# Operand loads of attention backward: larger pieces, requested by SP instead of GpSimd

## The chip, the cores and the metric

The program runs on one core of a Trainium2 chip. The metric is the device time of one execution in microseconds (us), lower is better. TensorE is called PE, VectorE DVE, ScalarE ACT, GpSimd POOL and SyncE SP, as in the profile. PE, DVE, ACT and POOL compute; SP here only requests DMA transfers.

## The reference

The kernel computes the output and nine gradients of a transformer block with adaptive layer norm (2048 tokens, width 512, 32 heads of 16, feed-forward width 1792), bfloat16 in and out. The part that matters here is the backward pass of the attention:

```
scores = einsum('bhqd,bhkd->bhqk', q, k) * scale
p = softmax(scores, axis=-1)
o = einsum('bhqk,bhkd->bhqd', p, v)
_out, _vjp = jax.vjp(_f, A_x, A_wqkv, A_wo, B_w1, B_b1, B_w2, B_b2, c, w_mod)
_grads = _vjp(grad_out)
```

For each head the backward pass forms P again from Q and K, dP from dO and V, then dS = P * dP (the row sums of dP are folded into two extra columns of dO and V), and from these dV = P^T dO, dK = dS^T Q and dQ = dS K.

## The kernel before

The program has a forward part with the feed-forward block and its backward mixed in (to about 1165 us in the profile), the attention backward `attn_bwd` (about 1165 to 2390 us, lines 1431 to 1655), and a last part for the projection gradients (`phase6`). The change lies in `attn_bwd`.

**Loops.** The 32 heads are 8 quads `g` of four heads. A quad is worked off as two pairs of heads, `jp` = 0 and 1, so there are 16 pairs. In a pair, `c` runs over four chunks of 512 keys and `ib` over 16 blocks of 128 queries, in groups of `G` = 4 blocks (`ib0`): 16 groups in a pair, 256 in all. For each block and each of the two heads `a`, PE computes the scores `st` (line 1608), ACT takes their exponential into `pu` (1611), PE computes `dp` (1522) one block late, and DVE multiplies the two into `ds` (1526). In some groups one of the eight products of a group goes over ACT to POOL instead (1540, 1541).

**The transposes.** dQ needs `ds` transposed. When a group of four blocks has its `ds`, SP requests one crossbar transfer for it (`dma_start_transpose`, line 1549, in `dS`): a [128 x 4096] bfloat16 tile, 1 MB, from SBUF to SBUF into one of five buffers `dsT` (one of them is a part of the tile `keep`). In every fourth group PE turns 4 of the 32 blocks itself (1565), and 28 are left to the transfer. PE reads two groups of transposed `ds` together, in `dq` (line 1484, accumulator `accq`): `dq` items wait in the list `pendq` until more than eight are there, so the two groups k and k+1 are read from the start of group k+4 on, two items after every even block. PE's instructions are in an order written by hand and are run in that order, and so are those of SP and POOL.

**The loads.** The operands of the next pair or quad are read from DRAM while the current pair is worked on. `load_group(g)` (1391) gives the pieces for a quad: `QT` and `dOT` (features on the partitions, 32 partitions for a head, of which 16 or 18 hold data), and `K`, `Q`, `dO` (tokens on the partitions). `pair_pieces(g, jp)` (1423) gives the four pieces for a pair, of K and V, which go into the tile `kvm` (`masked`). `load_wmt` and `wq_pieces` give pieces of weights for the last part. In the last pair 16 pieces of `xhat1` are loaded. Half of a quad's pieces belong to each of its two pairs.

The list `pieces` of a pair is spread evenly over its 16 groups. This is the place, lines 1594 to 1597:

```
while pieces and ((total - len(pieces)) * SC * ST <= m * G * total or m == SC * ST // G - 1):
    if last:
        nc.gpsimd.tensor_copy(tick[:], last[7][0:1, 0, 0, 0:1])
    nc.gpsimd.dma_start(*pieces.pop(0))
```

`m` is the group's number in the pair, and `last` the block before. The copy to `tick` reads one element of the `ds` of the group before, so that POOL does not run ahead with the loads. The first loads of all, for the first pair, are requested by SP at line 933, ahead of `attn_bwd`.

Of the kernel before, what the change touches and what calls it, by code (L numbers as in the profile page):

```python
# [19 lines left out]
P = 128  # L20
DH = 16
# [4 lines left out]
def chunks(total, size):  # L26
    out = []
    s = 0
    while s < total:
        w = min(size, total - s)  # L30
        out.append((s, w))
        s += w
    return out
# [72 lines left out]
class K:  # L106
# [1284 lines left out]
    def load_group(self, g):  # L1391

        S, ST, qp = self.S, self.ST, self.qp
        tm = {"K": self.ktm_d, "Q": self.qtm_d, "dO": self.dOp_d}
        fm = {"QT": (self.QTq_d, DH), "dOT": (self.dOTq_d, DH + 2)}
        width = {n: S if n in fm else ST * P if n == "K" else ST * 4 * DH for n in (*fm, *tm)}
        if g < 2:
            T, o = {}, 0
            for n, e in width.items():
                if g:  # L1400
                    T[n] = qp.tile([P, e], BF16, name=f"{n}g")[:]
                elif n == "K":
                    T[n] = self.keep[:, :e]
                else:
                    T[n] = self.q0[:, o:o + e]
                    o += e
            self.Tq[g] = T
        T, pieces = self.Tq[g % 2], []
        for n, (src, rows) in fm.items():
            if g < 2:  # L1410
                pieces += [(T[n][:, s0:s0 + sw], src[g, :, s0:s0 + sw]) for (s0, sw) in chunks(S, 1024)]
            else:
                pieces += [(T[n][r:r + rows, :], src[g, r:r + rows, :]) for r in range(0, P, 32)]
        for n, src in tm.items():
            pieces += [(T[n][:, a:a + 256], src[g, :, a:a + 256]) for a in range(0, width[n], 256)]
        return {n: t if n in fm else t.rearrange("p (st w) -> p st w", st=ST) for n, t in T.items()}, pieces

    def wq_pieces(self, t):
# [3 lines left out]

    def pair_pieces(self, g, jp):
        pieces = []
        for n, src, sh, rows in (("KT", self.KTq_d, 0, DH), ("VT", self.VTq_d, 2, DH + 2)):
            for j in (2 * jp, 2 * jp + 1):
                r = 32 * ((j + sh) % 4)
                pieces.append((self.masked[n][j % 2][r:r + rows, :], src[g, r:r + rows, :]))
        return pieces

    def attn_bwd(self):
# [7 lines left out]
        tc, nc = self.tc, self.nc  # L1439
# [24 lines left out]
        def turn(g, jp, kvT, s0):  # L1464

            if kvT is None:
                return turn_q(g, jp)
            h0 = 4 * g + 2 * jp
            n = ST // 2
            tp = stp.tile([P, n, P], BF16, name="st")  # L1470
            for st in range(n):
                nc.tensor.transpose(tp[:, st, :], kvT[:, (s0 + st) * P:(s0 + st + 1) * P], self.ident[:])
            v = tp[:].rearrange("p s (t a e) -> p t s a e", t=2, a=2)
            for t, dst in enumerate((self.dk_t, self.dv_t)):
                d = dst[:, s0:s0 + n, h0 * DH:(h0 + 2) * DH].rearrange("p s (a d) -> p s a d", a=2)
                nc.scalar.copy(d, v[:, t, :, :, 0:DH])
# [40 lines left out]
        def dP(u, a):  # L1517

            (T, g, jp, c, ib, kvT, pu, dsg, i, grp) = u
            rd = slice(64 - 64 * jp, 128 - 64 * jp)  # L1520
            dp = dpp.tile([P, 512], F32, name="dp")
            nc.tensor.matmul(dp[:], lhsT=T["dOT"][rd, ib * P:(ib + 1) * P],  # L1522
                             rhs=masked["VT"][a][rd, 512 * c:512 * (c + 1)], start=True, stop=True)
            if a == 1 and i == 1 and off(c, ib):
                return dp
            nc.vector.tensor_tensor(dsg[:, i, a], dp[:], pu[:, a, :], ALU.mult)  # L1526

        def odd(c, ib):
            return (c * SC + ib // G) % 2 == 1

        def no_turn(c, ib):
            return ib // G > 0
# [4 lines left out]
        def dP_pool(u, dp):  # L1537
            (T, g, jp, c, ib, kvT, pu, dsg, i, grp) = u
            f = (self.junk6, self.csq)[(c * SC + ib // G) % 2]
            nc.scalar.copy(f[:], dp[:])  # L1540
            nc.gpsimd.tensor_tensor(dsg[:, i, 1], f[:], pu[:, 1, :], ALU.mult)  # L1541
# [23 lines left out]
                nc.tensor.transpose(tp[:, b, :], dsg[:, 0, 0, b * P:(b + 1) * P], self.ident[:])  # L1565
            nc.scalar.copy(dsT[:, 0:4 * P], tp[:].rearrange("p b k -> p (b k)"))

        tick = self.tick
        wmt = self.load_wmt()
        T = self.T0  # L1570
        last = None
        for g in range(NQ):
            for jp in range(2):
                if jp == 0:
                    if g + 1 < NQ:
                        Tn, later = self.load_group(g + 1)
                    else:
                        Tn, later = None, self.wq_pieces(1) + wmt[2 * g + 1:]
                    cut = len(later) // 2 if Tn else len(later)
                    pieces = self.pair_pieces(g, 1) + wmt[2 * g:2 * g + 1] + later[:cut]  # L1580
                    later = wmt[2 * g + 1:2 * g + 2] + later[cut:]
                elif g + 1 < NQ:
                    pieces = self.pair_pieces(g + 1, 0) + later
                else:
                    pieces = [(self.xhat1_6[:, st, :], self.xhat1_d.rearrange("(st p) d -> p st d", p=P)[:, st, :])
                              for st in range(ST)]
                kvT = kvp.tile([P, S], BF16, name="kvT")
                end = (g, jp) == (NQ - 1, 1)
                total = len(pieces)
                for c in range(SC):  # L1590
                    c0 = 512 * c
                    for ib0 in range(0, ST, G):
                        m = c * (ST // G) + ib0 // G
                        while pieces and ((total - len(pieces)) * SC * ST <= m * G * total or m == SC * ST // G - 1):
                            if last:
                                nc.gpsimd.tensor_copy(tick[:], last[7][0:1, 0, 0, 0:1])
                            nc.gpsimd.dma_start(*pieces.pop(0))
                        dsg, grp = self.dsp.tile([P, G, 2, 512], BF16, name="ds"), []
                        for i in range(G):
                            ib = ib0 + i  # L1600
                            q = slice(ib * P, (ib + 1) * P)
                            if turnq and i == 3 and m >= (7 if turnq[0][2] is None else 2):
                                turn(*turnq.pop(0))
                            pu = self.pup.tile([P, 2, 512], BF16, name="pu")
                            for a in range(2):
                                stt = stp.tile([P, 512], F32, name="st")
                                rs = slice(64 * jp, 64 * jp + 64)
                                nc.tensor.matmul(stt[:], lhsT=T["QT"][rs, q], rhs=masked["KT"][a][rs, c0:c0 + 512],  # L1608
                                                 start=True, stop=True)
                                held = dP(last, a) if last else None  # L1610
                                nc.scalar.activation(pu[:, a, :], stt[:], ACT.Exp, scale=self.scale)  # L1611
                                if held is not None:
                                    dP_pool(last, held)
                                if a == 0 and i % 2 == 1 and odd(c, ib) and len(pend) >= 4:
                                    kv_two(1)
                            if last:
                                dS(last)
                            last = (T, g, jp, c, ib, kvT, pu, dsg, i, grp)
                            if i % 2 == 1 and len(pend) >= 4:
                                kv_two(1 if odd(c, ib) else 2)  # L1620
                            elif i % 2 == 0 and len(pendq) > 2 * G:
                                for _ in range(4 if end else 2):
                                    dq(pendq.pop(0))
                            if i == 2:
                                turn_ds(dsg, grp, no_turn(c, ib), end and m > 2)
            T = Tn
# [339 lines left out]
```

## Time and profile before

| | |
|---|---|
| time, median of 3 runs | 2515.87 us (2509.63 to 2516.81) |
| span of the profiled execution | 2498.5 us |
| median less span | 17.4 us |
| attention backward in the profile | about 1165 to 2390 us |
| busy share of the whole span | PE 96%, ACT 91%, DVE 68%, POOL 30% |
| crossbar transfers of `ds` (line 1549) | 256 |
| loads at line 1597, copies to `tick` at line 1596 | 260 and 259 |

The span runs from the first to the last instruction of one profiled execution; the time of a run also holds what lies around it, here 17.4 us against the median. In the rows below, `PE accq L1484 <- DMA dsT<-ds` means that the instruction on PE that writes `accq` at line 1484 waited for the DMA that writes `dsT` from `ds`. SPq and POOLq are the queues of requests on SP and POOL. The row of a DMA request on SP lasts as long as SP is held by it; the transfer lands later, and "DMA to landing" counts from the request's start. q1 is the hardware queue that SP uses, q0 the software queue of POOL.

### The profile page before, as it was taken

The numbers are of one execution on the slowest core, as the hardware profiler recorded it, in microseconds if no ns is written. First come the engines' busy times: TensorE is split into PE (matmuls) and PEld (weight loads), VectorE is DVE, ScalarE is ACT, GpSimd is POOL, SyncE is SP. The second block draws the span as 40 slices with busy tenths as digits, with TensorE's granted clock in tenths as the row PEclk, the third lists the DMA queues.
The fourth block names the chain that finished last, engine by engine and source line by source line (L and its number), as shares of the span: only waits on it lengthen the run. The fifth ranks groups of instructions, "written<-read, shape, count | busy, mean of one in ns | idle before, by whom it ended". The sixth has DMA issues, their size and how long they took to land.

```text
span 2498.5 us, 67897 instructions
## 1 busy us (share of the span) xinstructions
PE 2410.2 (96%) x26211; PEld 1061.6 (42%) x26439; DVE 1695.0 (68%) x3487; ACT 2283.1 (91%) x3757; POOL 753.5 (30%) x1337
## 2 busy tenths in 40 slices
PE   8999999999999999999999999999999999999998
PEld 4555555555555555583233332333333333333343
DVE  6222322422332343576999999999999999999957
ACT  7999999999999997534999999999999999999945
POOL 2344531220131022245222323322333222322223
PEclk9999999999999999999999999999999999999999
DMA  4589661541243045499999999999999999999997
GB/s 166 135 179 208 169 125 47 132 100 40 92 114 98 23 123 147 110 199 216 232 235 233 232 227 231 237 234 231 230 235 239 234 230 236 234 233 236 238 217 192
DMA packets 1293547, 454.13 MB, mean 182 GB/s; under 512 B 1236948, under 2 KB 1261398, under 8 KB 1293222
## 3 DMA queue, kind: packets, MB, share of 16 engines
q1 hardware_dynamic: 1252422, 344.68, 71.8%
q0 software_dynamic: 38720, 104.04, 13.9%
q8 instruction: 207, 3.39, 0.6%
q10 hardware_dynamic: 2080, 1.05, 0.2%
q14 instruction: 118, 0.97, 0.1%
HBM read 75.83 MB, written 64.49 MB: 56 GB/s over the span
## 4 chain that ended last, share of the span: by engine, by line
PE 49%; ACT 35%; DMA 7%; issue 5%; DVE 3%; POOL 1%; SPq 1%; ACTq 0%; DVEq 0%; POOLq 0%
ACT pu L391 26%; PE st L1608 17%; PE acckv L1459 8%; ACT pu L1611 6%; DMA dsT<-ds 5%; PE accq L1484 5%; PE st L388 4%; PE dp L1522 2%; PE accbank L322 2%; PE dps L1050 2%; PE dp L1659 1%; PE st L1754 1%; ACT csq L1540 1%; PE pps L1237 1%; DVE ds L1526 1%
## 5 line engine op out<-in xcount | busy, mean ns | idle before, releaser
L1526 DVE TENSOR_TENSOR ds<-dp,pu 128x512 bf16<-128x512 f32 x1888 | 1166.0, 682 | 34.6 <-PE dp L1522 19.1
L1611 ACT ACTIVATE pu<-st 128x512 bf16<-128x512 f32 x2048 | 1073.8, 666 | 34.7 <-PE st L1608 21.3
L391 ACT ACTIVATE pu<-st 128x1024 bf16<-128x1024 f32 x992 | 912.1, 1077 | 4.2 <-PE st L388 3.7
L388 PE MATMUL st<-QTm,KTq 128*128 128x512 bf16 x1859 | 560.9, 377 | 27.1 <-ACT pu L391 6.1
L322 PEld LDWEIGHTS <-pu 128*128 128x128 bf16 x8192 | 346.7, 96 | 236.1 <-issue 3.0
L1522 PE MATMUL dp<-kvm,q 64*128 64x512 bf16 x1024 | 365.0, 384 | 2.0 <-DVE ds L1526 0.7
L322 PE MATMUL accbank<-Vaug,pu 128*128 128x17 bf16 x8192 | 357.4, 171 | 8.3 <-ACT Vaug L522 1.1
L1522 PE MATMUL dp<-kvm,dOTg 64*128 64x512 bf16 x1024 | 363.6, 383 | 0.3
L1608 PE MATMUL st<-kvm,q 64*128 64x512 bf16 x1024 | 349.4, 382 | 5.4 <-ACT pu L1611 0.2
L1608 PE MATMUL st<-kvm,QTg 64*128 64x512 bf16 x1024 | 348.1, 381 | 6.5
L1541 POOL TENSOR_TENSOR ds<-csq,pu 128x512 bf16<-128x512 f32 x128 | 147.2, 1150 | 627.0 <-ACT csq L1540 553.6
L388 PEld LDWEIGHTS <-KTq 128*128 128x128 bf16 x1984 | 188.4, 96 | 176.9 <-issue 124.8
L1459 PE MATMUL acckv<-ds,Qg 128*16 128x512 bf16 x1024 | 176.2, 382 | 0.3
L1459 PE MATMUL acckv<-pu,q 128*16 128x512 bf16 x1024 | 176.3, 383 | 0.0
L1459 PE MATMUL acckv<-ds,q 128*16 128x512 bf16 x1024 | 176.2, 383 | 0.0
L1459 PE MATMUL acckv<-pu,dOg 128*16 128x512 bf16 x1024 | 176.0, 382 | 0.0
L302 POOL DMA_DIRECT2D QTm<-QTq_d x124 | 63.1, 511 | 341.5 <-PE st L388 320.0
L1608 PEld LDWEIGHTS <-q 64*128 64x128 bf16 x1024 | 67.0, 94 | 163.5 <-issue 150.6
L1608 PEld LDWEIGHTS <-QTg 64*128 64x128 bf16 x1024 | 67.1, 94 | 160.6 <-issue 145.7
L329 DVE RECIPROCAL rl<-accbank 128x4 f32<-128x4 f32 x128 | 22.9, 179 | 158.3 <-PE accbank L322 158.2
L1522 PEld LDWEIGHTS <-q 64*128 64x128 bf16 x1024 | 88.8, 93 | 52.9 <-issue 43.3
L1522 PEld LDWEIGHTS <-dOTg 64*128 64x128 bf16 x1024 | 88.2, 93 | 52.9 <-issue 43.8
(390 smaller groups left out, 3055.1 us busy)
## 6 DMA issues: line engine op xcount, KB each, us to landing
KTq<-KTq_d POOLq DMA_DIRECT2D x24, 512.0 KB, 3.9
duT_d<-auT POOLq DMA_DIRECT2D x3, 1792.0 KB, 7.9
aT_d<-rT POOLq DMA_DIRECT2D x3, 1792.0 KB, 11.5
KTq_d<-KTq SPq DMA_DIRECT2D x32, 128.0 KB, 2.1
QTq_d<-ev_fm SPq DMA_DIRECT2D x32, 128.0 KB, 4.3
ktm_d<-ev_tm POOLq DMA_DIRECT2D x32, 128.0 KB, 2.5
VTq_d<-vT POOLq DMA_DIRECT2D x4, 1024.0 KB, 6.3
dx<-dx_d SPq DMA_DIRECT2D x16, 256.0 KB, 4.6
```

The source lines that it names most:

```text
L302: nc.gpsimd.dma_start(QTm[j][32 * j:32 * j + 32, :], self.QTq_d[g, 32 * j:32 * j + 32, 512 * qc:512 * (qc + 1)])
L322: nc.tensor.matmul(acc[:, a, sub, :], lhsT=pu[:, a, sub * P:(sub + 1) * P], rhs=Vaug[:, kb, h, :], start=(kb == 0 and a == 0 and sub == 0) ...
L388: nc.tensor.matmul(stt[:, a, :], lhsT=KT[:, kb * P:(kb + 1) * P], rhs=QTm[2 * jp + a][:], start=True, stop=True)
L391: nc.scalar.activation(pu[:], stt[:], ACT.Exp, scale=self.scale)
L1050: nc.tensor.matmul(pt[:], lhsT=a[st], rhs=g_tm[:, st, :], start=(st == 0), stop=(st == ST - 1))
L1459: nc.tensor.matmul(acckv[r:r + DH, :], lhsT=T[n][:, ib, col:col + DH], rhs=src[:, a, :], start=(ib == 0), stop=(ib == ST - 1))
L1484: nc.tensor.matmul(accq[r:r + 32, o:o + 256], lhsT=T["K"][:, 4 * c + sub, col:col + 32], rhs=v[:, r // 32 % 2 * 2:r // 32 % 2 * 2 + 2, 4 * ...
L1522: nc.tensor.matmul(dp[:], lhsT=T["dOT"][rd, ib * P:(ib + 1) * P], rhs=masked["VT"][a][rd, 512 * c:512 * (c + 1)], start=True, stop=True)
L1526: nc.vector.tensor_tensor(dsg[:, i, a], dp[:], pu[:, a, :], ALU.mult)
L1541: nc.gpsimd.tensor_tensor(dsg[:, i, 1], f[:], pu[:, 1, :], ALU.mult)
L1608: nc.tensor.matmul(stt[:], lhsT=T["QT"][rs, q], rhs=masked["KT"][a][rs, c0:c0 + 512], start=True, stop=True)
L1611: nc.scalar.activation(pu[:, a, :], stt[:], ACT.Exp, scale=self.scale)
```

## The change

The loads of lines 1594 to 1597 are requested by SP, so they stand in the same queue as the crossbar transfers. The copy to `tick` is gone: the place in SP's order now holds a load back. The pieces are larger: `K`, `Q` and `dO` in 1024 columns instead of 256 (for quads 1 to 7), `QT` and `dOT` (quads 2 to 7) in two pieces instead of four. Since such a piece now spans two heads, it also reads the unused partitions between them: 48 rows for `QT` instead of two times 16, 64 for `dOT` instead of two times 18. The V pieces have 32 rows instead of 18. There are 152 loads instead of 260.

```
-        fm = {"QT": (self.QTq_d, DH), "dOT": (self.dOTq_d, DH + 2)}
+        fm = {"QT": (self.QTq_d, 32 + DH), "dOT": (self.dOTq_d, 64)}
...
-                pieces += [(T[n][r:r + rows, :], src[g, r:r + rows, :]) for r in range(0, P, 32)]
+                pieces += [(T[n][r:r + rows, :], src[g, r:r + rows, :]) for r in range(0, P, 64)]
         for n, src in tm.items():
-            pieces += [(T[n][:, a:a + 256], src[g, :, a:a + 256]) for a in range(0, width[n], 256)]
+            pieces += [(T[n][:, a:a + w], src[g, :, a:a + w]) for a, w in chunks(width[n], 1024 if g else 256)]
...
-        for n, src, sh, rows in (("KT", self.KTq_d, 0, DH), ("VT", self.VTq_d, 2, DH + 2)):
+        for n, src, sh, rows in (("KT", self.KTq_d, 0, DH), ("VT", self.VTq_d, 2, 32)):
...
-        tick = self.tick
...
-                            if last:
-                                nc.gpsimd.tensor_copy(tick[:], last[7][0:1, 0, 0, 0:1])
-                            nc.gpsimd.dma_start(*pieces.pop(0))
+                            nc.sync.dma_start(*pieces.pop(0))
```

The order of PE, ACT and DVE is the same in both kernels. SP's and POOL's change. These are SP's requests at the start of pair (g, jp) = (3, 0) before, only crossbar transfers into the buffers `dsT` and `keep`:

```order
L1549 DMA_TRANSPOSE keep<-ds 128x32x128
L1549 DMA_TRANSPOSE dsT_19897<-ds 128x32x128
L1549 DMA_TRANSPOSE dsT_19898<-ds 128x28x128
L1549 DMA_TRANSPOSE dsT_19899<-ds 128x32x128
L1549 DMA_TRANSPOSE dsT_19900<-ds 128x32x128
L1549 DMA_TRANSPOSE keep<-ds 128x32x128
L1549 DMA_TRANSPOSE dsT_19897<-ds 128x28x128
```

And SP at the same place now (line 1597 of before is 1594 here); `kvm` takes the K and V pieces of the next pair:

```order
L1549 DMA_TRANSPOSE keep<-ds 128x32x128
L1594 DMA kvm<-KTq_d 16x2048
L1549 DMA_TRANSPOSE dsT_19897<-ds 128x32x128
L1549 DMA_TRANSPOSE dsT_19898<-ds 128x28x128
L1594 DMA kvm<-KTq_d 16x2048
L1549 DMA_TRANSPOSE dsT_19899<-ds 128x32x128
L1549 DMA_TRANSPOSE dsT_19900<-ds 128x32x128
L1594 DMA kvm<-VTq_d 32x2048
L1549 DMA_TRANSPOSE keep<-ds 128x32x128
L1549 DMA_TRANSPOSE dsT_19897<-ds 128x28x128
```

A load now stands ahead of about every second crossbar transfer, right behind the one before. On POOL, at the same place before, pairs of a copy and a load stood between the products of line 1541 (`csq` holds what ACT copied there):

```order
L1541 TENSOR_TENSOR ds<-csq,pu 128x512
L1596 COPY tick<-ds 1x1
L1597 DMA kvm<-KTq_d 16x2048
L1596 COPY tick<-ds 1x1
L1597 DMA kvm<-KTq_d 16x2048
L1541 TENSOR_TENSOR ds<-csq,pu 128x512
L1596 COPY tick<-ds 1x1
L1597 DMA kvm<-VTq_d 18x2048
```

Now POOL has the products alone in the attention backward:

```order
L1541 TENSOR_TENSOR ds<-junk_19880,pu 128x512
L1541 TENSOR_TENSOR ds<-csq,pu 128x512 x6
L1541 TENSOR_TENSOR ds<-junk_19880,pu 128x512
L1541 TENSOR_TENSOR ds<-csq,pu 128x512 x2
L1541 TENSOR_TENSOR ds<-junk_19880,pu 128x512
```

All copies and loads have left POOL's order there, and the order of its products is kept.

## The prediction

> **What bounds the kernel now.** I read the busy times by stretch first. The columns are the stretch, its length, PE's busy time with its instructions, the granted clock, the DMA share and GB/s.
>
> ```profile
> 1165.00:1250.00 85.00, 79.52 (x766) 0.98 1.05 212
> 1250.00:1400.00 150.00, 148.45 (x1618) 1.00 1.21 234
> 1400.00:1550.00 150.00, 146.52 (x1580) 1.00 1.21 229
> 1550.00:1700.00 150.00, 148.09 (x1608) 1.00 1.23 236
> 1700.00:1850.00 150.00, 148.22 (x1608) 1.00 1.21 232
> 1850.00:2000.00 150.00, 147.75 (x1604) 1.00 1.22 236
> 2000.00:2150.00 150.00, 148.63 (x1610) 1.00 1.20 233
> 2150.00:2300.00 150.00, 148.37 (x1618) 1.00 1.21 232
> 2300.00:2385.00 85.00, 82.18 (x889) 1.00 1.20 239
> sum 1220.00, PE 1197.72; mean PE 133.08
> ```
>
> PE is busy in 1197.7 of 1220.0 us. The change moves no instruction of PE, ACT or DVE, so it can take away at most the 22.3 us in which PE stands still, 0.9% of the time. The DMA engines are never quiet either. Next, the waits of PE in this stretch (total, times, longest), and what the crossbar requests look like on SP:
>
> ```profile
> PE accq L1484 <- DMA dsT<-ds: 7.4, 12, 2.9
> PE dp L1522 <- DVE ds L1526: 0.7, 3, 0.3
> ```
>
> ```profile
> L1549 SPq DMA_TRANSPOSE dsT<-ds x208: 3490/4262/6457, 1173.4 to 2377.8; - x104
> L1549 SPq DMA_TRANSPOSE keep<-ds x48: 3550/4204/5392, 1192.2 to 2300.7; - x48
> DMA to landing us min/median/max: 5.1/7.2/9.0
> ```
>
> Of PE's idle time only 7.4 us are put down to a DMA: PE wants a transposed tile that has not landed, twelve times. The 256 requests start (2377.8 - 1173.4) / 255 = 4.72 us apart, and a median one holds SP for 4.26 us of that. So SP and the transfers behind it run nearly as full as PE.
>
> The longest wait shows what happens. These are single requests on SP, one from each of four short windows, then PE at 1217, the chain of waits there, and POOL's loads just before:
>
> ```profile
> 1173.45 3.53 SPq L1549 DMA_TRANSPOSE dsT<-ds  x1
> ...
> 1187.45 4.03 SPq L1549 DMA_TRANSPOSE dsT<-ds  x1
> ...
> 1206.13 5.37 SPq L1549 DMA_TRANSPOSE dsT<-ds  x1
> ...
> 1211.60 6.46 SPq L1549 DMA_TRANSPOSE dsT<-ds  x1
> ```
>
> ```profile
> 1217.22 0.40 PE L1484 MATMUL accq<-dsT,keep 128*32 128x256 bf16 x6 [2.90 <-DMA dsT<-ds]
> ```
>
> ```profile
> 1206.13 11.04 DMA dsT<-ds
> ```
>
> ```profile
> 1195.98 0.59 POOL L1597 DMA_DIRECT2D QTg<-QTq_d  x1
> ...
> 1197.78 0.54 POOL L1597 DMA_DIRECT2D QTg<-QTq_d  x1 [0.26 <-issue]
> ...
> 1204.86 0.58 POOL L1597 DMA_DIRECT2D dOTg<-dOTq_d  x1
> ...
> 1207.00 0.54 POOL L1597 DMA_DIRECT2D dOTg<-dOTq_d  x1 [0.26 <-issue]
> ```
>
> Undisturbed, 32 blocks (1 MB) hold SP 4.03 us and 28 blocks 3.53. While POOL's loads of 256 KB run (128 x 1024 bfloat16), the same request takes 5.37 and then 6.46 us. The tile requested at 1206.13 came after 11.04 us, and PE had waited 2.90 of them, so it was due 11.04 - 2.90 = 8.1 us after its request. The median landing is 7.2 us. **The spare time is thus about 0.9 us**, and whatever delays one transfer by more makes PE wait.
>
> **The change part by part.** *POOL.* 259 copies and 260 requests go away. PE gains nothing from that, since POOL's products wait for ACT, not for POOL:
>
> ```profile
> POOL ds L1541 <- ACT csq L1540: 553.6, 115, 8.1
> ...
> POOL kvm L1597 <- PE dp L1522: 8.5, 25, 0.6
> ```
>
> ```profile
> L1596 POOL COPY tick<-ds 1x1 bf16<-1x1 bf16 x259 | 45.7, 177 | 106.6 <-DVE ds L1526 106.6
> ```
>
> The copies are 45.7 us of work on an engine that is 30% busy. Value 0.
>
> *Bytes.* A normal first pair of a quad now has nine loads: two K pieces of 64 KB (16 rows of 4 KB), two V pieces of 128, 96 of weights, two of QT of 192, two of dOT of 256: 1376 KB. Over all 152 loads the shapes add up to 23424 KB, against 19632 KB in 260 before, 19% more. At the crossbar's own 4.03 us per 1024 KB, 1376 KB is 5.4 us of transfer in a pair.
>
> *SP.* What a plain load costs on SP shows at line 933, where SP itself loads the first pair (min/median/max in ns):
>
> ```profile
> L933 SPq DMA_DIRECT2D kvm<-KTq_d x2: 354/378/402, 1140.1 to 1140.5; - x2
> L933 SPq DMA_DIRECT2D kvm<-VTq_d x2: 368/399/430, 1140.9 to 1142.9; - x2
> L933 SPq DMA_DIRECT2D q<-QTq_d x2: 357/510/664, 1143.4 to 1151.6; - x2
> L933 SPq DMA_DIRECT2D q<-dOTq_d x2: 443/606/769, 1152.3 to 1155.0; - x2
> ```
>
> Nine loads: 2 x 0.38 + 2 x 0.40 + 0.4 + 2 x 0.51 + 2 x 0.61 = 4.2 us of SP. A pair lasts 16 x 4.72 = 75.5 us, and its 16 transfers undisturbed hold SP for 12 x 4.03 + 4 x 3.53 = 62.5. The loads add between 4.2 us (the requests alone) and 4.2 + 5.4 = 9.6 us (if the transfer time is paid on SP as well): 66.7 to 72.1 us. Before, the contention with POOL's loads was already in SP's rows: 16 x 4.26 = 68.2. So SP does not run full on the average, at either end. I take 62.5 + 5.4 + 1 = 69, about as before, since a request is made while the queue still has work.
>
> The Trainium skill, Perfetto Trace Analysis, section "DMA Instruction — HWDGE (DVE, Sync)", says that such a row runs until the descriptors are made and that the data movement is not in it; by that alone a load would cost SP its own row and the pair would need the 66.7. The rows above differ: the same request took 4.03 us and 6.46 us, so here a full queue is in the row.
>
> *One load ahead of one transfer.* SP has 4.72 - 4.03 = 0.69 us free in a group. A 256 KB load costs between 0.51 us (the lower of its two median rows) and 0.61 + 1.0 = 1.6 us; I take 1.0, its transfer time. The transfer behind it is then 0.3 us late, less than the 0.9 us to spare, and nine loads in 16 groups leave a free group behind most of them, in which 0.69 us are won back. Queued behind the load are all later transfers, and PE waits for those. The four loads that caused the 2.90 us wait now stand at groups 9, 11, 13 and 15 and not four in eleven us.
>
> *Waits on SP.* A load of K waits for the last scores of the pair before, which PE runs before SP comes to that request; POOL's requests waited there for at most 0.6 us. 0, at most 2 x 0.6 in a pair, which the free time takes up.
>
> *Sum.* Of the 7.4 us the 2.9 go, and of the other 4.5 (eleven waits of 0.4 us) I let about half go: -5 us. Span 2498.5 - 5 = 2493.5; with the 17.4 us around it 2511 us against 2515.87, or -0.2%. That is below 0.3%, about what a measurement of this kernel can tell from no change.
>
> **The rivals.** *The queue does not catch up (slower).* If a large load costs more than the 2 x 0.69 = 1.38 us that SP wins back until the next, the lag grows over the second half of each pair. For it speak the rows of the last part, where SP has loads of 256 KB between smaller transposes:
>
> ```profile
> 2394.08 1.36 SPq L1737 DMA_TRANSPOSE dqT<-dv_t  x1
> ...
> 2437.72 1.03 SPq L1741 DMA_DIRECT2D dx<-dx_d  x2
> 2438.84 1.24 SPq L1737 DMA_TRANSPOSE dqT<-dk_t  x1
> 2440.13 4.08 SPq L1737 DMA_TRANSPOSE dqT<-dv_t  x1
> ```
>
> Two loads take 1.03 us, and the second transpose behind them 4.08 instead of 1.36: (1.03 + 2.72) / 2 = 1.9 us for one. Four such loads leave 4 x 0.5 = 2 us at the pair's end, 1.1 beyond the spare time, in 14 pairs 16 us; the last pair has a load of 128 KB in each group, at half of 1.9 less 0.69 = 0.26 us each 4 us more: 2536. Against it: POOL's loads run in that stretch too, and may be what the 4.08 us shows.
>
> *Nothing changes (2516).* The same 16 DMA engines move the same bytes and a fifth more, and PE's late tiles stay late for the transfer time, not for the requester. The Trainium skill, DMA: Bandwidth & Descriptors, section "Issuing engines are not separate DMA queues", says just this: requests from any engine interleave on the same engines, and only time on the requester is saved. By that rule the time stays. The trace agrees so far that loads from POOL slow SP's transfers.
>
> *All of it goes (faster).* If the transfers pace the loop in ways that no wait shows, PE's idle time from 1250 to 2300 us, 1050 - 1036.0 = 14 us, goes with the 2.9: 2516 - 17 = 2499. For it: SP is held 4.26 of 4.72 us, and the profile puts waits of SP down to the copy that goes:
>
> ```profile
> SPq L1549 <- DVE ds L1526: 440.0, 182, 5.8
> SPq L1549 <- POOL tick L1596: 313.9, 149, 5.3
> ```
>
> ```profile
> 1195.87 0.18 POOL L1596 COPY tick<-ds 1x1 bf16<-1x1 bf16 x1
> ```
>
> ```profile
> 1196.63 4.56 SPq L1549 DMA_TRANSPOSE dsT<-ds  x1
> ```
>
> Against it: here the copy ended at 1196.05, 0.58 us before the request that is said to have waited for it, so DVE's last product released it; and only 7.4 us of PE's waits name a DMA.
>
> **How the numbers follow.** Forecast (2508 to 2514): 0.49, of which 0.10 beyond -0.3%. Nothing: 0.15. All of it: 0.18. Slower: 0.18. Faster by over 0.3% is then 0.18 + 0.10 = 0.28, within 0.3% is 0.39 + 0.15 = 0.54, slower 0.18. The likeliest time is 2511; the range reaches half into the faster rival and half into the slower one, 2503 to 2528.
>
> **What would show it.** Right: the waits of PE for `dsT` fall from 7.4 to about 3 us and the 2.9 us wait near the start is gone; the undisturbed 4.03 us becomes the usual row at line 1549; a load's row on SP is 0.4 to 1.0 us; the requests at line 1549 come 4.70 us apart. Wrong: rows of line 1549 behind a load of 6 us and more, waits for `dsT` that gather at the ends of the pairs (the slower rival), or waits that stay at 7 us (nothing).

## The result and the profile after

The changed kernel takes 2535.64 us (median of 4 runs, 2532.37 to 2540.76), the kernel before beside it 2512.75 us (4 runs, 2509.32 to 2516.81): a ratio of 1.0101 with a 95% interval of 1.0077 to 1.0125. It is slower by 23 us. The prediction, 2511 us in a range up to 2528, was wrong.

The profiled execution after has a span of 2530.6 us at a time of 2532.37 us. In each of its four runs the time is only 1.8 us above the span. The 17.4 us that the prediction took as lying around the span of before were thus mostly another thing: its profiled execution was faster than the median of the runs. The spans of the two pages differ by 32.1 us, the medians by 22.9, and some 9 us of what the two traces show is this difference between executions.

**The crossbar transfers.** Line 1549 after (min/median/max in ns, first and last start):

```profile
L1549 SPq DMA_TRANSPOSE dsT<-ds x208: 3515/4238/8600, 1171.2 to 2409.0; - x104
L1549 SPq DMA_TRANSPOSE keep<-ds x48: 3509/4172/5563, 1190.0 to 2329.7; - x48
...
DMA to landing us min/median/max: 5.2/6.5/9.8
```

They start (2409.0 - 1171.2) / 255 = 4.85 us apart instead of 4.72 before. These 0.13 x 255 = 33 us are the whole difference of the spans, so all of it is in the attention backward. The rows on SP did not become shorter (median 4.24 us for 4.26). From request to landing, however, a transfer is now faster, 6.5 us for 7.2. What is late is the request. This is SP over 38 us (start, duration, request; x2 are two in a row):

```profile
1437.38 4.27 SPq L1549 DMA_TRANSPOSE dsT<-ds  x1
1441.70 0.57 SPq L1594 DMA_DIRECT2D keep<-ktm_d  x1
1442.37 8.19 SPq L1549 DMA_TRANSPOSE dsT<-ds  x2
1450.60 0.57 SPq L1594 DMA_DIRECT2D keep<-ktm_d  x1
1451.28 5.68 SPq L1549 DMA_TRANSPOSE dsT<-ds  x1
1457.06 4.20 SPq L1549 DMA_TRANSPOSE keep<-ds  x1
1461.32 0.57 SPq L1594 DMA_DIRECT2D q<-qtm_d  x1
1461.98 8.54 SPq L1549 DMA_TRANSPOSE dsT<-ds  x2
1470.58 0.58 SPq L1594 DMA_DIRECT2D q<-dOp_d  x1
1471.27 4.43 SPq L1549 DMA_TRANSPOSE dsT<-ds  x1
```

Each row begins within 0.12 us of the end of the one before: SP has no free time here. Over the whole stretch, 231 of 255 transfers start within 0.25 us of the end of the request ahead of them; before it was 124. A load adds its row of 0.57 us and a second gap of about 0.1 us:

```profile
L1594 SPq DMA_DIRECT2D kvm<-KTq_d x30: 502/528/577, 1162.9 to 2262.2; - x30
...
L1594 SPq DMA_DIRECT2D q<-dOTq_d x6: 582/590/601, 1382.9 to 2016.8; - x6
```

A piece of 16 KT rows (64 KB) and one of 64 dOT rows (256 KB) hold SP almost equally long, 0.53 and 0.59 us.

**Where PE pays.** The waits of PE in the attention backward (total, times, longest; the row of `dp` after `ds` had 0.7 us before):

```profile
PE accq L1484 <- DMA dsT<-ds: 16.9, 18, 2.1
PE dp L1522 <- DVE ds L1526: 10.0, 15, 1.5
PE accq L1484 <- DMA keep<-ds: 2.3, 4, 1.2
```

The waits for transposed tiles rose from 7.4 to 16.9 + 2.3 = 19.2 us. Of the 10 us for `ds`, 5.8 come from the same transfers by another way: the `ds` buffers are read by the transfers, and in six places DVE had to wait for the late transfer out of a buffer before it could write it. For the other 4.2 us the profile names ACT, PE or nothing ahead of DVE's product, so their cause is not shown. First the chain of waits at one of the six places, then DVE and PE there:

```profile
1394.02 8.23 DMA dsT<-ds
...
1402.37 0.70 DVE ds L1526
```

```profile
1402.37 3.25 DVE L1526 TENSOR_TENSOR ds<-dp,pu 128x512 bf16<-128x512 f32 x5 [1.71 <-DMA dsT<-ds]
```

```profile
1403.11 0.37 PE L1522 MATMUL dp<-kvm,dOTg 64*128 64x512 bf16 x1 [1.44 <-DVE ds L1526]
```

DVE stood 1.71 us for the transfer, and PE 1.44 us for DVE. Two microseconds after PE goes on, something follows that the prediction did not have: PE's granted clock falls to half. These four stretches (length, PE busy, clock, DMA share, GB/s) are all such stretches of the attention backward; the last one follows a wait of 1.38 us for `ds` that the profile puts down to ACT. Before there was one, behind the 2.90 us wait at 1217.

```profile
1405.10:1408.50 3.40, 3.40 (x29) 0.50 1.23 280
1715.70:1719.10 3.40, 3.40 (x26) 0.50 1.26 286
1876.10:1879.50 3.40, 3.40 (x30) 0.51 1.17 265
2258.40:2261.80 3.40, 3.40 (x24) 0.51 1.30 228
```

Half a clock for 3.4 us costs 1.7 us of PE. The sum: waits named above 8.1 us before and 29.2 after, 21 us more; three half-clock stretches more, 5 us. That is 26 of the 32 us between the spans, but the account is not closed. From the first transfer's request to the last one's, all of PE's idle time, short gaps included, rose from 21 to 39 us, by 18, and its busy time by 16, of which the clock explains 5. Some 10 us are in no row that I can name.

ACT shows why it may all count. ACT's busy time from 1250 to 2300 us, before and then after:

```profile
sum 1050.00, ACT 1041.17; mean ACT 148.74
```

```profile
sum 1050.00, ACT 1017.89; mean ACT 145.41
```

ACT was busy 99% of the time before, more than PE. PE, ACT and DVE feed one another with hardly any slack, so a stall of PE is hardly won back.

### The profile page after: what moved, and what is told of

Read it like the earlier page. It is cut to its first block, busy times and chain, and to the rows that moved or that the text cites. A ratio compares the mean times of both kernels' runs of the same rounds, so it can differ in the third digit from the quotient of the medians.

```text
span 2530.6 us, 67538 instructions
## 1 busy us (share of the span) xinstructions
PE 2441.3 (96%) x26439; PEld 1060.4 (42%) x26439; DVE 1696.3 (67%) x3487; ACT 2290.9 (91%) x3757; POOL 583.5 (23%) x818
## 4 chain that ended last, share of the span: by engine, by line
PE 54%; ACT 24%; DMA 13%; issue 5%; DVE 3%; POOL 1%; SPq 1%; POOLq 0%; DVEq 0%; ACTq 0%
ACT pu L391 17%; PE st L1605 14%; PE st L388 8%; DMA dsT<-ds 8%; PE acckv L1459 7%; ACT pu L1608 5%; PE accq L1484 5%; PE accbank L322 3%; DMA keep<-ds 2%; PE dp L1522 2%; PE dps L1050 2%; PE pps L1237 2%; PE st L1751 1%; PE pps L631 1%; DVE ds L1526 1%
## 5 line engine op out<-in xcount | busy, mean ns | idle before, releaser
L388 PE MATMUL st<-QTm,KTq 128*128 128x512 bf16 x1984 | 587.5, 377 | 19.6 <-ACT pu L391 6.1
L1605 PEld LDWEIGHTS <-q 64*128 64x128 bf16 x1024 | 66.9, 94 | 163.6 <-issue 150.9
L329 DVE RECIPROCAL rl<-accbank 128x4 f32<-128x4 f32 x128 | 22.9, 179 | 159.1 <-PE accbank L322 158.8
L1484 PE MATMUL accq<-dsT,keep 128*32 128x256 bf16 x1632 | 108.2, 279 | 11.6 <-DMA dsT<-ds 11.4
L1484 PE MATMUL accq<-dsT,Kg 128*32 128x256 bf16 x1696 | 102.1, 278 | 5.5 <-DMA dsT<-ds 5.4
```

The lines of the kernel that those rows point to most:

```text
L388: nc.tensor.matmul(stt[:, a, :], lhsT=KT[:, kb * P:(kb + 1) * P], rhs=QTm[2 * jp + a][:], start=True, stop=True)
L1484: nc.tensor.matmul(accq[r:r + 32, o:o + 256], lhsT=T["K"][:, 4 * c + sub, col:col + 32], rhs=v[:, r // 32 % 2 * 2:r // 32 % 2 * 2 + 2, 4 * ...
```

## Experiments

My theory after the result was that SP's queue is full. The rival: the pieces themselves (19% more bytes, larger loads) delay the transfers, whichever engine requests them. All ratios are to the kernel before, run on the same chip.

### One part of the change at a time

**pieces_on_gpsimd**: the nine pieces, requested as before.

```
-                            nc.sync.dma_start(*pieces.pop(0))
+                            if last:
+                                nc.gpsimd.tensor_copy(self.tick[:], last[7][0:1, 0, 0, 0:1])
+                            nc.gpsimd.dma_start(*pieces.pop(0))
```

> The nine larger pieces stay, but GpSimd requests them behind the copy, as before the change; SP requests only crossbar transfers. Theory (SP's queue is full: a load costs its own row of 0.57 us with a gap of 0.12, and lengthens the crossbar rows behind it by 0.74, 1.43 in all, and nine or ten of these in a pair take the free time): SP is free again, 2510 to 2520 us, requests at line 1549 some 4.72 us apart. Rival (bytes and sizes: 19% more bytes, in larger pieces, are what delays the crossbar transfers): the time stays at 2530 to 2540.

Measured: 2531.92 us, ratio 1.0082 (1.0054 to 1.0109). The rival is right: the pieces alone cost almost what the whole change costs. But they cost it in another way. The chain of waits, POOL and PE at one of the longest waits:

```profile
1689.39 10.96 DMA dsT<-ds
```

```profile
1690.04 0.56 POOL L1596 DMA_DIRECT2D q<-dOTq_d  x1 [0.29 <-issue]
```

```profile
1700.38 0.40 PE L1484 MATMUL accq<-dsT,Kg 128*32 128x256 bf16 x6 [3.05 <-DMA dsT<-ds]
```

A dOT piece of 256 KB is requested 0.65 us after a transfer, and the transfer lands after 10.96 us instead of 7.4 (its median here). PE waits 3.05 us, and its clock then falls to half. Of 256 transfers 18 land more than 9 us after their request; in the changed kernel, where the loads stand between the transfers in one queue, it is 2, and before 3.

**small_on_sp**: the 17 small pieces of before, requested by SP.

```
-                            if last:
-                                nc.gpsimd.tensor_copy(tick[:], last[7][0:1, 0, 0, 0:1])
-                            nc.gpsimd.dma_start(*pieces.pop(0))
+                            nc.sync.dma_start(*pieces.pop(0))
```

> The 17 small pieces of before (260 loads, 19632 KB), but requested by SP at the places of the change. Theory (SP's queue): 260 loads x (0.69 us + 0.74 x 75.5/154 = 0.36) = 1.05 us each, 17.1 in a pair instead of 9.5 x 1.43 = 13.6; with the 4.85 us of a group as the base this is 3.5/16 = 0.22 us more a group, so 2565 to 2595 us. Rival (bytes and sizes): the old bytes in the old sizes, 2510 to 2520 us.

Measured: 2548.65 us, 1.0150 (1.0124 to 1.0177). Here the rival is wrong (it said 2510 to 2520), and my size was too large. The transfers are 4.90 us apart:

```profile
L1549 SPq DMA_TRANSPOSE dsT<-ds x208: 3426/4118/8983, 1178.2 to 2428.1; - x104
```

I had not reckoned that the rows of the transfers shrink (median 4.12 us), presumably because the queue drains during the loads' rows. So both parts of the change are harmful alone, by 22 and by 39 us, and together they cost 23.

**pieces_on_act**: the nine pieces requested by ACT, `nc.scalar.dma_start(*pieces.pop(0))`, without the copy.

> The nine larger pieces, at the same places of the program, but requested by ScalarE and so on a hardware queue of its own. Theory (SP's queue): SP's rows of line 1549 come 4.72 us apart if ScalarE lets them; but ScalarE is busy 1196 of 1220 us, so if a load costs it the 0.57 us that it costs SP, 152 of them are 87 us, about 60 more than it has to spare: 2565 to 2580; if a load costs it 0.1 us or less, 2512 to 2520. Rival (bytes and sizes): 2530 to 2540 or more, with the waits of PE for dsT as after the change.

Measured: 2539.30 us, 1.0120 (1.0076 to 1.0164), in neither of the two ranges of the theory and in the rival's. ACT mostly pays 0.31 to 0.51 us for a load, as in this row, less than SP:

```profile
1271.63 0.31 ACTq L1594 DMA_DIRECT2D q<-QTq_d  x1
```

PE waits for transposed tiles a little less than with the same pieces on GpSimd (22.0 us for 27.3), and one transfer took 14.0 us to land:

```profile
PE accq L1484 <- DMA dsT<-ds: 21.6, 15, 5.6
```

But the run shows less than it seems, since on ACT the loads don't stand where they did. The 16 pieces of weights, which the change requests from 1203 to 2324 us, are all requested ahead of the attention backward:

```profile
L1594 ACTq DMA_DIRECT2D WmT<-WmT_d x16: 326/390/1224, 1070.7 to 1107.7; - x16
```

Of the 152 loads 105 follow the one before within 5 us; in the change it is 21. What of the 29 us is ACT's own time, what the bunching and what the collisions was not parted.

**loads_left_out**: the change without the loads of KT, VT, QT, dOT, K, Q, dO that are requested in quads 1 to 6 of the loop; 56 loads remain of 152. The later quads then compute with the operands of earlier ones, so only the time means anything.

```
-                            nc.sync.dma_start(*pieces.pop(0))
+                            p = pieces.pop(0)
+                            if g in (0, NQ - 1) or p[0].shape[1] == 384:
+                                nc.sync.dma_start(*p)
```

> The change, but the loads of the attention operands (KT, VT, QT, dOT, K, Q, dO) of quads 2 to 7 are left out, so that later quads compute with the operands of the first two; the weights and the last pairs' loads stay. It shows what all these loads cost together. Theory and rival both: SP is free, PE's waits for dsT, keep and ds (19 and 10 us) go, 2500 to 2508 us. If loads cost nothing and the order of the program does, it stays at 2535.

Measured: 2504.51 us, 0.9978 (0.9963 to 0.9994). Without two thirds of the loads the kernel is 0.2% faster than before. Any other way to make these loads can hardly bring more. ACT is the likely reason; its busy time there from 1250 to 2300 us:

```profile
sum 1050.00, ACT 1044.94; mean ACT 149.28
```

### What the requests cost on SP

**halves_on_gpsimd** and **halves_on_sp**: the rows and bytes of the change, each piece cut into two column halves that are spread over the pair's groups. The diff is the same for both; the first kernel requests the halves by GpSimd behind the copy, the second by SP.

```
+                pieces = [(d[:, a:a + d.shape[1] // 2], s[:, a:a + d.shape[1] // 2])
+                          for d, s in pieces for a in (0, d.shape[1] // 2)]
                 total = len(pieces)
```

> The rows and bytes of the change (23424 KB), but each piece cut into two halves of its columns, 304 requests spread evenly over the groups of a pair and made by GpSimd behind the copy. With whole pieces GpSimd took 2532 us: 18 of 256 crossbar transfers landed more than 9 us after their request, where before it was 3. Theory (size): one load of 192 to 256 KB in one request delays the transfer that it meets past the 8.1 us at which PE needs it, and one of half the size does not: 2510 to 2518 us, and about 5 transfers over 9 us. Rival (bytes): 19% more bytes delay the transfers however they are cut: 2527 to 2535.

> The same 304 halves, spread the same way, requested by SP. Theory (requests of SP): the crossbar transfers land early after their request (small pieces on SP: 2 of 256 over 8.1 us) but are requested late, since each load holds SP for 0.57 us and a gap of 0.07 to 0.12; 304 x 0.63 = 191 us of gaps and 40 more between requests, with crossbar rows of 1068 to 1113 us in sum, are 1300 to 1345 us, 5.1 to 5.3 us a group: 2595 to 2640 us. Rival (bytes): as the change, 2532 to 2540.

Measured: 2514.97 us on GpSimd, 1.0019 (0.9995 to 1.0043), and 2582.39 us on SP, 1.0274 (1.0233 to 1.0315). The same loads, and 67 us between the two requesters. On GpSimd 304 loads with the 19% more bytes cost nothing that is sure and at most 0.4%, so the bytes as such are not the main cause. On SP, with the same bytes, 304 loads cost 47 us more than the change's 152. SP there:

```profile
1405.51 1.23 SPq L1596 DMA_DIRECT2D q<-dOTq_d  x2
1406.85 4.25 SPq L1549 DMA_TRANSPOSE dsT<-ds  x1
1411.14 0.58 SPq L1596 DMA_DIRECT2D kvm<-KTq_d  x1
1411.84 3.94 SPq L1549 DMA_TRANSPOSE dsT<-ds  x1
1415.87 0.53 SPq L1596 DMA_DIRECT2D kvm<-KTq_d  x1
1416.49 3.57 SPq L1549 DMA_TRANSPOSE dsT<-ds  x1
```

A load stands ahead of every transfer, and the group takes about 5 us though the transfers are at their shortest. That loads on SP are paid by their number is shown. The number of rows in memory doubled as well, but SP's own row of a load hardly depends on it: it is 0.53 us for 16 rows and 0.57 for 128. What of the price is SP's own time and what the hardware queue behind it was not parted. My 2595 to 2640 was again too much, for the same reason as with the small pieces.

**wide_columns_on_gpsimd** and **wide_columns_on_sp**: the kernel before with K, Q and dO alone in 256 KB pieces (176 loads, bytes as before), requested by GpSimd and by SP.

```
-            pieces += [(T[n][:, a:a + 256], src[g, :, a:a + 256]) for a in range(0, width[n], 256)]
+            pieces += [(T[n][:, a:a + w], src[g, :, a:a + w]) for a, w in chunks(width[n], 1024 if g else 256)]
```

> The kernel before with one part of the change: K, Q and dO in pieces of 1024 columns (256 KB) instead of 256 (64 KB); QT, dOT and VT stay in pieces of 16 or 18 rows; GpSimd and the copy stay. Theory (size): these loads were met by transfers that landed after 8.2 us in the mean and 9.8 at most, so only some make PE wait: 2514 to 2524 us. Rival (only the row pieces matter): 2508 to 2514. Rival (bytes): the bytes are those of before, 2508 to 2514.

> The kernel before with K, Q and dO in pieces of 256 KB (harmless on GpSimd) and QT, dOT, VT in pieces of 16 or 18 rows, 176 loads and 19632 KB, requested by SP. From 152 to 304 loads of the same bytes on SP the time rose by 47 us, 0.31 us a load; 260 loads with 19632 KB took 2549, where 152 + 108 x 0.31 would give 2569, so 3.8 MB less are worth about 20 us. Theory (SP's queue is full: requests and bytes count): 2536 + 24 x 0.31 - 20 = 2523, from 2518 to 2528 us. Rival (on SP too only the tall pieces do harm): 2508 to 2513. Rival (requests alone): 2540 to 2546.

Measured: 2508.11 us on GpSimd, 0.9985 (0.9967 to 1.0003), no difference, where my theory had 2514 to 2524; 2529.28 us on SP, 1.0075 (1.0053 to 1.0098). With harmless pieces the way over SP alone costs 21 us. The estimate of 2523 from requests and bytes was 6 us too low and its range just missed, and the rival that only the tall pieces matter on SP is out.

**ahead_of_even_only**: the change with its loads placed only ahead of the first tile of each two that PE reads together.

```
-                        while pieces and (
+                        while pieces and m % 2 and (
```

> The change, with its loads issued at odd groups only, some groups with two. PE reads the transposed tiles in pairs, so a load then stands ahead of a pair's first tile, which has a group more time, and never directly ahead of its second. Theory (SP's queue is full, so a delay is carried on to all later transfers): 2532 to 2542 us. Rival (it is the one transfer behind the load that is late): 2515 to 2524.

Measured: 2540.23 us, 1.0122 (1.0096 to 1.0148). Giving the delayed transfer a group more of time brings nothing. The requests are as far apart as in the change, (2418.5 - 1179.9) / 255 = 4.86 us:

```profile
L1549 SPq DMA_TRANSPOSE dsT<-ds x208: 3489/4222/9797, 1179.9 to 2418.5; - x104
```

A delay is not absorbed by the one transfer behind a load but carried on to those after it.

### What in the pieces harms on GpSimd

**tall_rows_on_gpsimd**: the kernel before with the other part of the pieces, QT in 48, dOT in 64 and VT in 32 rows.

```
-        fm = {"QT": (self.QTq_d, DH), "dOT": (self.dOTq_d, DH + 2)}
+        fm = {"QT": (self.QTq_d, 32 + DH), "dOT": (self.dOTq_d, 64)}
...
-                pieces += [(T[n][r:r + rows, :], src[g, r:r + rows, :]) for r in range(0, P, 32)]
+                pieces += [(T[n][r:r + rows, :], src[g, r:r + rows, :]) for r in range(0, P, 64)]
...
-        for n, src, sh, rows in (("KT", self.KTq_d, 0, DH), ("VT", self.VTq_d, 2, DH + 2)):
+        for n, src, sh, rows in (("KT", self.KTq_d, 0, DH), ("VT", self.VTq_d, 2, 32)):
```

> The kernel before with the other part of the change: QT in pieces of 48 rows, dOT of 64, VT of 32 (4 KB a row), with the 19% more bytes that this brings; K, Q and dO stay in pieces of 256 columns; GpSimd and the copy stay. Theory (size): a dOT piece of 256 KB was met by transfers that landed after 9.0 us in the mean and 10.95 at most, the worst of all pieces, so most of the 22 us come from here: 2520 to 2530 us. Rival (bytes): all of the 22 us, 2529 to 2535.

Measured: 2535.44 us, 1.0096 (1.0063 to 1.0128), above both ranges. All of the loss of the pieces on GpSimd is in these.

**rows_of_v_gpsimd** changes only the last line of that diff, **qt_dot_gpsimd** only the first two places.

> The kernel before with VT alone in pieces of 32 rows (128 KB, 30 loads) instead of 18 (72 KB); everything else as before, on GpSimd. Theory (only the pieces of 192 and 256 KB of QT and dOT do harm): 2508 to 2514 us. Rival (V's pieces have their share of the 25 us, as pieces of 128 KB into 32 partitions): 2516 to 2524.

> The kernel before with QT in pieces of 48 rows and dOT of 64 (24 loads for 48), V as before in 18 rows, on GpSimd. Theory (the tall pieces of QT and dOT do the harm): 2525 to 2535 us. Rival (V's pieces, or the sum of both): 2512 to 2520.

Measured: 2512.83 us, 1.0009 (0.9988 to 1.0030) for V, and 2535.48 us, 1.0103 (1.0081 to 1.0126) for QT and dOT. So it is the 24 loads of QT and dOT. PE's waits with them:

```profile
PE accq L1484 <- DMA dsT<-ds: 21.3, 17, 2.8
PE accq L1484 <- DMA keep<-ds: 6.1, 4, 2.7
```

Five kernels then changed the shape of these pieces. **tall_in_two_gpsimd** (the nine pieces on GpSimd, QT and dOT as two column halves requested directly one after the other):

```
+                            dst, src = pieces.pop(0)
+                            n = 2 if dst.shape[0] in (48, 64) else 1
+                            w = dst.shape[1] // n
+                            for a in range(0, n * w, w):
+                                nc.gpsimd.dma_start(dst[:, a:a + w], src[:, a:a + w])
```

> The nine pieces of the change requested by GpSimd behind the copy (2532 us as whole pieces), but each QT piece of 48 rows and dOT piece of 64 is requested as two column halves one directly after the other: the same bytes at the same places, in rows of 2 KB instead of 4 KB. Wide pieces (128 rows of 2 KB, 256 KB) cost nothing, tall ones all of the 22 us. Theory (row length): 2 KB rows are harmless, 2508 to 2516 us. Rival (few partitions, or 256 KB into 64 partitions at once): 2526 to 2536.

**qt_dot_col_halves** (the same halves, but as pieces of their own) and **tall_by_rows_gpsimd** (cut by rows instead):

```
+                pieces = [(d[:, a:a + w], s[:, a:a + w]) for d, s in pieces
+                          for w in (d.shape[1] // 2 if d.shape[0] in (48, 64) else d.shape[1],)
+                          for a in range(0, d.shape[1], w)]
```

```
+                pieces = [(d[a:b], s[a:b]) for d, s in pieces
+                          for a, b in (((0, 32), (32, d.shape[0])) if d.shape[0] in (48, 64) else ((0, d.shape[0]),))]
```

> The nine pieces of the change on GpSimd, with QT and dOT alone cut into column halves (48 and 64 rows of 2 KB) that spread over the groups as pieces of their own; K, Q, dO stay 256 KB and V 32 rows. Cut by rows it was 2524 us, and with all pieces halved 2515. Theory (128 KB at a time is harmless in rows of 2 KB): 2510 to 2517. Rival (V in 32 whole rows, or the number of loads of 128 KB and more, keeps the loss): 2520 to 2530.

> The nine pieces of the change on GpSimd, but QT and dOT pieces are cut by rows (32 and 16, 32 and 32 rows of 4 KB), as pieces of their own that spread over the groups of the pair; K, Q and dO stay 256 KB. Theory (row length): rows of 4 KB stay, so 2522 to 2532 us. Rival (at most 128 KB to 64 partitions at a time is harmless): 2510 to 2518.

**all_rows_gpsimd** (the kernel before with QT and dOT in two pieces of all 128 rows) and **rows_of_32_gpsimd** (with half of their small pieces padded to 32 rows):

```
-                pieces += [(T[n][r:r + rows, :], src[g, r:r + rows, :]) for r in range(0, P, 32)]
+                pieces += [(T[n][:, a:a + 1024], src[g, :, a:a + 1024]) for a in range(0, S, 1024)]
```

```
-                pieces += [(T[n][r:r + rows, :], src[g, r:r + rows, :]) for r in range(0, P, 32)]
+                pieces += [(T[n][r:r + rows, :], src[g, r:r + rows, :]) for r, rows in ((0, 32), (32, rows), (64, 32), (96, rows))]
```

> The kernel before with QT and dOT in two pieces each, as in the change, but cut by columns: 128 rows of 2 KB (256 KB) instead of 48 or 64 rows of 4 KB; V, K, Q and dO as before, on GpSimd. With the tall pieces it was 2535 us. Theory (a piece that goes into 64 partitions or fewer delays the crossbar transfers, one that goes into all 128 does not, as the wide pieces of K, Q and dO showed): 2508 to 2516 us, although it is more bytes than the tall pieces. Rival (256 KB of QT or dOT in any shape): 2526 to 2536.

> The kernel before with four pieces for each of QT and dOT as before, but two of each four padded from 16 or 18 rows to 32 (128 KB); all rows are 4 KB, on GpSimd. Theory (amount at a time into few partitions): 128 KB is half of what did harm, 2508 to 2516 us, as V's 32 rows showed. Rival (rows of 4 KB above 72 KB do harm, as the cut by rows at 2524 hinted): 2518 to 2526.

| QT and dOT requested by GpSimd as | K, Q, dO | us | ratio |
|---|---|---|---|
| 16 or 18 rows of 4 KB (before) | 64 KB | 2512.75 | 1 |
| half of them 32 rows of 4 KB | 64 KB | 2520.03 | 1.0043 (1.0018 to 1.0068) |
| 128 rows of 2 KB | 64 KB | 2527.04 | 1.0070 (1.0053 to 1.0088) |
| 48 or 64 rows of 4 KB | 64 KB | 2535.48 | 1.0103 (1.0081 to 1.0126) |
| 48 or 64 rows of 2 KB, spread | 256 KB | 2512.55 | 1.0016 (1.0004 to 1.0027) |
| 48 or 64 rows of 2 KB, two at once | 256 KB | 2527.38 | 1.0068 (1.0042 to 1.0094) |
| 32 (16) rows of 4 KB, spread | 256 KB | 2523.96 | 1.0062 (1.0036 to 1.0087) |

(V has 32 rows in the last three kernels of the table and 18 in the others; by itself that cost 1.0009.) What holds in the table: how much of QT or dOT is in flight at once matters. The same halves cost 1.0016 spread and 1.0068 when two are requested at once. It is not all, since pieces of at most 128 KB cost 1.0062 when cut by rows, and 1.0043 where half of the small ones were padded to 32 rows. My theories of the shape fell: two halves of 2 KB rows at once are not harmless, nor are pieces over all 128 partitions, nor pieces of 128 KB as such. What stays open is why the cut by rows is worse than the cut by columns, and why 256 KB of K, Q or dO cost nothing in the sum where 256 KB of QT or dOT do. These pieces stand at other places of a pair, and that was not tried.

**all_rows_on_sp**: the change with QT and dOT in all 128 rows, as in the diff of all_rows_gpsimd.

> The change with QT and dOT as 128 rows of 2 KB instead of 48 or 64 rows of 4 KB: as many requests, still by SP. Theory (on SP it is the requests and the bytes that count, since the loads don't run beside the transfers): 2533 to 2543 us. Rival (the tall pieces do the harm on SP too): 2515 to 2526.

Measured: 2544.60 us, 1.0137 (1.0109 to 1.0165). It is just above the 2533 to 2543 of the theory. On SP the shape that is the milder one on GpSimd helps nothing, as the theory of the full queue has it.

No version beats the kernel before by more than can be measured. The best that computes everything is wide_columns_on_gpsimd, 0.9985 (0.9967 to 1.0003).

## Why the prediction was wrong

**The step that failed** is "One load ahead of one transfer": "The transfer behind it is then 0.3 us late, less than the 0.9 us to spare, and nine loads in 16 groups leave a free group behind most of them, in which 0.69 us are won back." It rested on the term for SP, "I take 62.5 + 5.4 + 1 = 69" of 75.5 us in a pair. In the trace after, the 256 rows of the transfers sum to 1113.0 us, 1113.0 / 16 = 69.6 in a pair, and 152 loads with about 0.57 + 0.14 us (their row, and the two gaps of 0.04 to 0.1 us around it) add 9.5 x 0.71 = 6.7. That is 76.3 us of the 77.7 that a pair now takes. My upper end, 72.1, was no upper end. The transfers did not go back to 62.5: they stayed at 69.6, probably because the loads' bytes now run in the same queue, and the loads' own rows came on top of that, at 0.57 us and not at the 4.2 / 9 = 0.47 of the nine rows at line 933. Even with most loads left out the 256 rows sum to 1065.8 us, 66.6 in a pair, so 62.5 was too low a base as well.

What a pair wins back was thus too little, and the trace shows it directly. Count the products of lines 1526 and 1541 in eights, one eight to a group, and take the time from the end of a group's last product to its transfer's request, as a mean over the pairs. Before, it is 0.1 to 0.3 us in every group. After, it is 0.6 to 1.3 us in groups 2 to 9 of a pair, and then it grows to 2.9 us in group 15; by group 2 of the next pair it is 0.6 again. The large loads stand ahead of the transfers of groups 8, 10, 12 and 14, and the first small one of the next pair ahead of that of group 15. The "0.3 us late" of the prediction did not stay with one transfer. The experiment with the loads ahead of first tiles only, and the two kernels of halves, agree with this.

**"Waits on SP"** held: SP waited for PE at line 1594 only 9.4 us in all, at most 0.6 at a time.

**"Bytes"** held as a count, 23424 KB, and the halves on GpSimd show that the 19% more cost little by themselves. What the prediction didn't ask is what one larger load does to the one transfer beside it. It took for granted that four loads of 256 KB at groups 9 to 15 are better than four in eleven us. The pieces alone on GpSimd cost 22 us.

**"POOL: value 0"** held as far as PE's order goes: no wait of PE for POOL appeared or went. The copy to `tick` was not taken away by itself, so what it is worth is not shown.

**"Sum"**: the wait of 2.9 us near the start did go, as forecast, and its half-clock stretch with it. But waits of 21 us came, and the sum had no term for the clock.

**The rivals.** *The queue does not catch up* gave 2536 us; it had 0.18. Its mechanism is the one that the trace shows: the lag grows over the second half of each pair, and the waits gather at the pair's end. Of the 29.2 us of waits above, 25.5 fall between group 8 of a pair and group 0 of the next, counted by the last transfer requested, only 1.4 in groups 1 to 7, and the rest behind the last transfer's request. Its prices were others. It gave a 256 KB load 1.9 us and most others nothing, while SP's row and gaps take about 0.7 us for any load, and it had no term for the clock. That its number came out so closely is in part chance. *Nothing changes* is refuted, and with it, for this kernel, the rule of the Trainium skill (DMA: Bandwidth & Descriptors, "Issuing engines are not separate DMA queues") as the prediction used it: the requester alone made 21 us for the wide pieces and 67 us for the halves. The rule names time on the requester as what is saved; here that time, 0.57 us a load, is much of what made the transfers late. *All of it goes* is refuted by loads_left_out: the transfers do not pace the loop of before. ACT, busy 99% of the time, is likely what paces it, but no run here made ACT's work shorter.

## What to carry to other kernels

Before a request is moved into a queue, add up the rows of that queue over a period, with the gaps between them: here the rows of before took 4.37 of 4.72 us a group (1119.8 us in 256 rows), and 0.6 loads of 0.7 us each were more than the rest. Then look at where in the period the loads stand, since the lag grows where they are dense and large. Fewer, larger loads are not cheaper by themselves: on GpSimd spread halves beat whole pieces here, while on SP, where each request is paid, the halves were the slowest kernel of all. Before anything is done about loads, leave them out once: here that showed 0.2% to gain.

## What the runs showed of the hardware that was not expected

**The clock after a short wait.** Waits of PE of 1.4 to 2.1 us were followed, 0.8 to 2 us after their end, by 3.41 us at half the granted clock, at four places of the changed kernel; halves_on_sp has 13 such stretches; other waits of the same length (1.45 us at 1537.9, 1.62 at 2182.1) were not. A wait of 1.4 us can so cost 3.1. The Trainium skill, TensorE: Matmul & The Clock Gate, section "Part 1: The HAM clock gate (the "warmup" mystery)", has the half rate and a window of 3413 ns that runs freely; the length of the stretches agrees. A free-running window agrees as well: the four stretches start 91, 47 and 112 times 3.413 us apart. If this is the window, each stretch is the window behind the one that held the wait, and the two waits that were not followed lie across the border of two windows, with at most 1.2 us in either. It does not explain all, since a wait of 1.46 us at 1327.0 lay within one window and was not followed. That the half rate needs an idle window of about 3.4 us, as its table has it, does not fit: these waits lasted 1.4 to 2.1 us, and the one before 2.9.

**The price of a request.** A plain load held SP for 0.53 us (64 KB) to 0.59 us (256 KB), and ACT mostly for 0.31 to 0.51 us.

**A shorter row is not a faster queue.** With 304 loads on SP the transfers' rows were the shortest of all kernels with loads in full (median 4.10 us for 4.26 before), and the kernel the slowest, so a short row does not say that the transfers come faster. My reading is that SP's rows hold the wait for room in its queue, and that this wait had only moved into the rows of the loads and the gaps.
